# New order, engine, slot and filler tables for a fixed list of 2793 steps: attention followed by a two-layer MLP on one Trainium2 core

## Chip, cores and metric

One core of a Trainium2 chip runs the whole program. The metric is device microseconds of one execution, given as the median of the runs; one further execution was taken by the hardware profiler, and all rows below are from it.

## What is computed

The input has batch 4, 8 heads, 576 positions and head size 64. A small network of 32 hidden units makes a bias from the distance of two positions; the bias is the same for all batches. The result of the attention goes, token by token (2304 tokens of width 512), through a layer of width 2048 with a leaky step.

```python
scores = scale * np.matmul(q, k.transpose(0, 1, 3, 2))
...
x = (psi_rel / psi_i)[..., None]
h = np.maximum(x @ w1 + b1, 0.0)
bias = h @ w2
scores = scores + bias.transpose(2, 0, 1)[None, :, :, :]
...
attn = np.exp(scores)
attn = attn / (np.sum(attn, axis=-1, keepdims=True) + 1e-09)
attn_out = np.matmul(attn, v)
...
h = x @ w_in
g = np.maximum(h, 0.0) + alpha * np.minimum(h, 0.0)
return (g @ w_out).astype(np.float32)
```

## The kernel before

**The work and its tiles.** The program is written as 2793 steps; a step is one instruction or a short run of them on one engine (a matmul group, an elementwise operation, a DMA).

- 36 bias tiles (`bias_tile`, L472). Each takes four relu images ("H" steps, on ACT L485, DVE L482 or POOL L488), one PE group (L503) into a PSUM tile S or O, one eviction ("ev", ACT L513 or DVE L514) and one DMA to a scratch in HBM (`scr`).
- Weight preparation (`weights`, `halves_of`): for each of eight pairs of hidden blocks the weights are loaded, their bits are put together on DVE (L679, L682), the maximum is found, and a high and a low f16 half are written. The same splitting is done to q, k (`qk_turn`, L586 on PE, then L592 on ACT and L593 on DVE, or L597 on either for batch 0) and v (`v_rows`).
- 32 attention units (`unit`): for two heads and a range of rows, scores on PE (L611 in f32 for batch 0, L612 in f16 for batches 1 to 3) into S or O, a minimum on DVE (L823), the exponential on ACT (L826), the row scale (L829, L831), the division (L846, L847 for batch 0; L836, L837 and L839 for the others), a transposition (PE L855 with ACT L865 for batch 0, a transposing DMA L842 into the tile `at` for the others), the product with v on PE into A (L884 or L876), and an eviction of A in two parts by ACT (L902) and DVE (L904) into `x`.
- Nine chunks of 256 tokens (`chunk`, `layer_pair`), each with eight pairs of hidden blocks: a first-layer group of 24 matmuls into H (L954), two ACT (L961) and two DVE (L962) steps that read H, a high and a low half of the result (L965, and L966 on DVE or L967 on POOL), and a second-layer group of 12 matmuls into O (L973). O gathers all pairs of an output group. Chunks 0 and 1 are split into four output groups each, the seven others are one group each: 15 output groups. The second-layer group of the last pair is two steps of six matmuls, one for each half of O, and each half is then read by one ACT or DVE step (L935, L936; L939 where it is added to an earlier group).

**PSUM.** O is one tile of two halves of 512 f32, S are two tiles of 1024 f32 (O also serves as a third S slot), A is one tile of 512 f32 and H one tile of two halves of 256 f32.

**What sets the order.** Nothing is decided at run time but the waits. `Planner.plan` takes three tables written out in the file. `ISSUE` lists the numbers of the steps in the order in which they are issued, each engine taking its own steps from it in this order; a suffix .1 or .2 picks the second or third engine of those that the step may run on. `SLOT` gives each of 1115 buffers the slot that it lies in. `IDLE` lists steps of PE with a number of filler matmuls (L1025, 512 columns, into H's tile) that are issued just ahead of them.

```python
for b, n in zip(bufs, SLOT.split(), strict=True):
    b.slot = int(n)
...
for x in ISSUE.split():
    n, a = (x + ".0").split(".")[:2]
    o = self.ops[int(n)]
    o.eng, _, o.alt = o.alts[int(a)]
```

The two halves of the last second-layer group and their readers are declared as apart from each other: step `t` of PE writes `(ob, t)`, and reader `t` waits for `(ob, t)`.

```python
for t in range(2):
    PE(lambda t=t: m2([t]), 1320, ky + 0.0015, [gg, w_s[fp, 1]], [(ob, t)])
```

Of the kernel before, what the change touches and what calls it, by code (L numbers as in the profile page):

```python
# [34 lines left out]
0 2 1 3 4 5 6 9 10 11 13 12 193 7 8 441 442 16 14 15 17 19 443 194 205 195 23 71.1 70.2 444 206 69 105 445 72.1 107 446 18 24 25 26 27 28 29 207 114  # L35
73 113.2 112.2 30 31 197 32 153 20 154 111 208 198 155 49 156 447 157 160 115 104 106.2 199 161 21 50 211 108 22 48 162 56.1 74 51.2 163 200 76.2 77
448 109 52 662 78 35 57.2 79.2 36 80 164 196 53 39 58.2 212 40.1 213 661.2 214 158 116 55 175 159 81 176 165 215 663 59 91.2 660 93.2 166.1 219 60 209
110 664 90.2 41.1 92 94 177 178 179 180 98 181 54 665.1 189 97.1 100 220 190 216 182 82 201 99.2 217 218 183 184 42 101 167 919 920 168 221 62.1 222
102 656 169 654 653 223 921 33 227.1 655.2 95.1 202 203 170 922 171 34 172 657 43.1 44 65 45 64.2 923 658 103 37 204 210 83 63.1 224 38 84.1 75 251 66
173 46 86.2 926 225 927 187 928 924 625.2 226 627.1 85 626.2 228 87 117 61 614 229 929 119 188.1 628.2 930 612.2 925 47 88.1 629 230 67 252 253 120.1  # L40
121 630 231 255 118 659 232 185 233 234 646 235 122 931 239 254 244 237.1 186 631 932 246 933 191 259 613 611.2 615 96 240 934 647 620.2 256 192 269
68 238 649 935 616 245 648.2 123.1 247 650 619.1 633.1 666 260 621.2 634.1 936 632 651 89 617 618.2 622 635 937 257 636 241 128 127.1 126 258 652 125
124 637 606 270 271 605.1 604 248 129 607.1 608 667 272 236 261 668 242 623 669 938 263 262 130 670.2 609.1 480 140.2 671 264 939 249.1 265 267.1 481
672.1 139 147.2 142 149 273 141.2 266 484 143 148 940 943 134 277 274 144 610 146.1 639 275 150 485 135 281 638 642.1 640.2 276 133 482 641.1 944 643
697 132.2 342 136 624 688 282 151 690 278 131 673 689 283 279 145 137.1 691.2 152 343 284 483 486.1 698.1 692 280 285.1 268 487 696.1 286 138 695.2
491 644 677.1 699 693.1 676 346 488 675 287 700 354 288 489 289 674.2 344 290 291 726 490 725.2 347 292 345 723.1 678 348 250 683.1 355 645 494 941
293 350 492 681 682.1 684 679 349 304 493 685 358.1 724 356 711.2 686 495 942 712 727 498 351 511 499 710.2 709.2 305 352 496 728 497 357 719 713 353
512 359 733.1 717.1 694 360 309 500 701 716 306 501 687 310 515 714 680 311 505 718 506 729 361 513 720 362 313 507.1 703.1 363 243 731.1 502 503 704
516 514 705 702 314 721 302.1 364 315 504 321 517.1 730 525 365 307 312 303 366 706 316 518 707 368 295 542 526 174 370 519 732.1 529 715 530 527 722
508 522 528 543 531.1 708 317 738.1 740 369 734 297 509 371.1 322 375 298 532 533 546 547 536 735 544 520 523 510 737 556 739.1 736 323 545 521 372  # L50
318 324 296 573 537 319 373 741 320 308 548.1 524 742 379 387 534 535 374 549 553 376 325.1 557 550 560 326 327 538 561 554 558 559 562.1 328 377 329
330 380 331 555 299 332 333 743 551 381 563 574 552 300 378 567 335 587 577 539 578 575 576 382 568 744 336 337 540 564 388 579.1 565 383 758 772 773
301 569 745 566 338 391.1 541 389 580 339 746 340 584 570 748 384 412 341 747 390 585 581 385 582 749 586 750.1 759 367 787 571 408 572 386 583 751
762 392 760 755 774 393 413 761 588 763 775 414 756 589 764.1 765 394 757 752 766 415 416 395 420 396 788 590 591 753 397 776 398 409 399 777.1 791
401 778 801 754 769 592 767 410 789 792 402 417 418 411 779 780 781 768 815 421 770 449 771 790 424.1 422 802 419 816 817 593.1 423 425 594 595 426
793.1 805 803 830 427 794 450 334 596 294 403 428 818 429 430 804 431 432 598 597 806 819 404.1 461 405 599 844 400 600 807.1 808 820 406 455 433 782
436 798 456 809.1 434 799 795.1 451 457 810 812.1 452 453 796 783 785 407 800 813 814 821 784 786 858 601 797 454 467 917 945 946 947 948 437 949 950
473 822.1 602 474 823 462 435 811.1 475 468 476 477 831 603 834 463 859 464 824 832 951 833 438 835 836 837 458 825 845 478 860 846 2150 841 828 952
838 848 957.1 839 459 826 842 953 954 955 847 861 469 956.1 849 850.1 851 958 982 460 829 862 827 918 959 960 873 843.1 2153 852 983 855 984 985 840
2151 887 853 961 962 963 901 2152 854 863.1 470 2154 856 864 874 2167 465 857 865.1 2158 2161 875 2155.1 2156.1 479 877 964 866 876 965 888 966 967  # L60
878 968 969 867.1 970 889 891 879.1 971 880 2159 868 2160 2162 2163 902 2164.1 890 892 972 973 893.1 976 1022 894 974 975 986 471 988 989 979 869 977
980 978 2170 881 884 898 439 895.1 1036 871 440 981 899 2171 2173 896 900.1 2172 2174 872 885 897 886 903 2175.1 1023 904 916 1024 2176.1 2178 1025
1026 1027 1028.1 882 1029 1037 2179 883 990 991 992 1330 1331 1332 1030 1333 466 2207 993.1 2157 1040 1334 1038 1337 1338 905 906 1055 2166 1031 1069
1339 907 908 987 2181 1041 909 2180 1039 1340 2182 2165 2169 2190 870 1033.1 994.1 1034 1042 2183.1 1043 1044.1 1045 472 1341 910 2191 1032 1047.1
1056 1057 1035 2193 2192 2168 911 1046 1059 1048 1070 2194 1335 1336 2195.1 1088 1071 912 2198 913 2177 1073 1356 914 1342 1102 2184.1 995.1 1060 2227
1058 1061 1062 2196.1 2201 1072 1074 1343 1075 1063.1 1357 2185 2187 1066.1 915 1116 1358 1359 1344 2199 1345 1049 1064 1089 1067 2188 2202 2200 1076
2203.1 1065 1346 1090 2186 2204 2189 1080.1 1092 2210 1117 1347 1348 2213 1132 1103 1081 1077.1 1093 1106 1068 1082 1118 2211 1104 1078 1050 1107 2214
1349 1091 2212 1079 1146 1105 1051 1133 1136 1052 2215.1 1053 1019 1108.1 1137 2218 1054 1109 1094.1 1095 1160 2221 1119 1134 2219 996 1099 2197 1100
1113.1 1161 2205 1096.1 2206 997 1114 1097 1101 1120 1121.1 1122 2222 2208 998 2209 1123.1 1147 1350 999 1000 1001 2220 1115 1002 1162 1083 1124
2216.1 1003 1110.1 1135 1004 1148 1098 1138 1005 1139 1360 1149 1006 1086 2232 1111 2223.1 1126 2233 1007 2235 1163 1140 1150 1013 1351 1125 1112 1141  # L70
1008 2217 1142 1361.1 1362 1151 2234 1152 1009 1143 2236 2224 2237 1084 1010 1144 2226 2240 1011 1363 1087 1164 1153 2225 2229 1165.1 1364 1154 1176
2238.1 1014 1157.1 1012 1016 2241 2243 1368.1 1365 1190 1158 1155 1366 1367 1085 1015 1017 1145 1166 2244 1018 2228 1352 1156 2231 1127 1167 1353 1177
1128 1130 1209 2242 1178 2239 1129 1223 1354 1168 1131 1355 2251 1369.1 1370 2254 1170 1180 1169 2245 1191 1371 2246 1372 1194 1393 1179 1430 1181
2252 2248 1159 1373 1182 1394 1374 1375 1376 1195 2250 1377 1378 2247 1379 1395 1183 2253 1380 1187.1 1184.1 1192 1384 1385 2255 1396 1242 1381 1188
2259 2256 2249.1 1382 1387 2260 2262 1386 1193 1189 1397 1185 1383 2261 2263 1399 1196.1 1400 2257 1210 1211 1401 1020 1402 1388 1212 2270 1213 1197
2264 1198 1398.1 1389 1390 1391 1405.1 1256 1171 1172 1392 1214 1403 1186 1739 1740 2265.1 1741 1201 1199 1742 1202 1224 1227 1215.1 1404 2271 2258
1225 1203 1743 1216 1200 2272 2273 1406.1 2274 1228 2275.1 1243 1226 1173 1246 1229.1 1746 1174 1230 1175 2278 1270 1247 1744.1 1407 1021 1244 2276.1
1234.1 1257 1408 1409 1217 1218 1220 1260 1410 1271 1411 1412 1413 1261 1221 2279 2281 2266 1219 1747 1748 1204 1245 1414 1415 1416 1248 1417 1749
1222 1272 1286 2267 1273 1249 1231 1205 2280 1274 2282 1421 1422 1232 2289 2292 1258 1233 1235 1750 1236 1207 1300 1423 2268 1424 1259 1418 1262.1
2269 1206 2290 1314 2293 2277 1263 2283 1419 1420 1275 1250.1 1765 1751.1 1208 2291 1427 2284 1752 2297 1251 1428 1425 1253 1237 1238 1429 1276 2298  # L80
# [997 lines left out]
```

## Time and profile before

| what | value |
|---|---|
| runs | 707.54, 706.51, 704.47 us; median 706.51 |
| profiled execution | 706.55 us, of which the span from first to last instruction is 704.8 |
| mean granted TensorE clock | 0.994 |
| busy share of the span | PE 95%, DVE 70%, ACT 57%, POOL 25% |
| filler matmuls | 112, busy 35.0 us, the last at 145.5 us |

PE busy includes the fillers. A row of a wait names the engine that waited, the step that waited by its output tile and line, and what released it.

### The profile page before, as it was taken

How to read it: one execution, taken by the hardware profiler on the slowest of the kernel's cores; microseconds unless marked ns; L12 is line 12 of the kernel's file. 1: busy time of each engine (PE TensorE's matmuls, PEld its weight loads, DVE VectorE, ACT ScalarE, POOL GpSimd, SP SyncE). 2: the span in 40 equal slices, each digit the busy share in tenths (PEclk: the TensorE clock that was granted, in tenths of full speed). 3: DMA queues.
4: the chain of work that ended last, by engine and by line, in shares of the span. 5: the costliest groups of instructions: out<-in, count | busy, mean ns of one | idle time of the engine just before them, and what ended most of it. 6: DMA issues, size and time to landing. Idle time of an engine off the chain costs nothing.

```text
span 704.8 us, 15254 instructions
## 1 busy us (share of the span) xinstructions
PE 668.1 (95%) x5728; PEld 422.9 (60%) x5728; DVE 495.7 (70%) x1214; ACT 400.5 (57%) x824; POOL 174.2 (25%) x235
## 2 busy tenths in 40 slices
PE   7998889989999989999999999999999999999997
PEld 2454435556755656566666666666566566666664
DVE  3799999998767878798867786777668556123342
ACT  3897999886667656646565565474546352121211
POOL 1544434431320221222213212322122212111000
PEclk9999999999999999999999999999999999999999
DMA  8998998767479899999999969998998844200000
GB/s 201 273 300 303 298 314 292 253 179 206 103 167 212 176 224 200 176 222 218 210 195 190 191 180 216 203 193 190 188 200 175 178 86 82 59 30 1 31 1 31
DMA packets 234342, 125.89 MB, mean 179 GB/s; under 512 B 202636, under 2 KB 202652, under 8 KB 234268
## 3 DMA queue, kind: packets, MB, share of 16 engines
q1 hardware_dynamic: 234136, 124.91, 77.1%
q8 instruction: 45, 0.74, 0.4%
q14 instruction: 29, 0.24, 0.1%
q10 hardware_dynamic: 132, 0.00, 0.0%
HBM read 73.88 MB, written 15.61 MB: 127 GB/s over the span
## 4 chain that ended last, share of the span: by engine, by line
PE 73%; DVE 11%; ACT 6%; issue 4%; DMA 4%; POOL 1%; SPq 0%; DVEq 0%; ACTq 0%; POOLq 0%
PE H L954 24%; PE O L973 24%; PE A L876 6%; PE S L612 5%; DVE fg L823 3%; PE A L884 2%; PE S L503 2%; PE S L586 2%; DMA at<-a 2%; PE S L611 1%; ACT at L485 1%; PE S L855 1%; DVE five L682 1%; ACT fg L513 1%; PE H L1025 1%
## 5 line engine op out<-in xcount | busy, mean ns | idle before, releaser
L954 PE MATMUL H<-x,win 128*128 128x256 f16 x1728 | 200.8, 273 | 1.4 <-DVE mg L962 1.2
L973 PE MATMUL O<-wout,mg 128*128 128x512 f16 x864 | 197.9, 379 | 2.6 <-DVE mg L939 1.2
L954 PEld LDWEIGHTS <-win 128*128 128x128 f16 x1728 | 166.7, 98 | 35.9 <-issue 8.1
L961 ACT ACTIVATE mg<-H,sm 128x256 f32<-128x256 f32 x144 | 63.9, 469 | 153.2 <-PE H L954 138.7
L973 PEld LDWEIGHTS <-mg 128*128 128x128 f16 x864 | 82.1, 98 | 95.6 <-issue 7.6
L962 DVE SCALAR_TENSOR_TENSOR mg<-H,sm,mg 128x256 f32<-128x256 f32 x144 | 65.9, 478 | 96.1 <-ACT mg L961 96.1
L826 ACT ACTIVATE fg<-fg,st 128x576 f32<-128x576 f32 x144 | 110.5, 769 | 32.9 <-DVE st L823 23.9
L823 DVE CUSTOM_DVE_ANT_0 fg<-S,fg 128x576 f32<-128x576 f32 x125 | 92.4, 750 | 15.9 <-PE S L612 15.0
L967 POOL TENSOR_TENSOR mg<-mg 128x512 f16<-128x512 f32 x39 | 46.9, 1203 | 158.0 <-DVE mg L965 67.0
L839 DVE SCALAR_TENSOR_TENSOR a<-fg,st,a 128x576 f16<-128x576 f32 x74 | 63.8, 865 | 22.7 <-ACT a L837 11.3
L836 POOL TENSOR_SCALAR a<-fg,st 128x576 f16<-128x576 f32 x42 | 34.0, 810 | 116.7 <-DMA at<-a 51.1
L612 PE MATMUL S<-qk 64*128 64x288 f16 (+1 forms) x684 | 54.9, 284 | 3.1 <-ACT at L865 1.6
L876 PE MATMUL A<-at,five 128*64 128x256 f16 (+3 forms) x720 | 51.6, 288 | 1.3 <-DVE x L904 1.3
L612 PEld LDWEIGHTS <-qk 64*128 64x128 f16 (+1 forms) x720 | 33.5, 96 | 22.8 <-issue 16.9
L876 PEld LDWEIGHTS <-five 128*64 128x64 f16 (+1 forms) x720 | 36.4, 109 | 14.9 <-issue 11.7
L829 POOL TENSOR_SCALAR st<-st 128x2 f32<-128x2 f32 (+1 forms) x48 | 14.5, 303 | 115.3 <-ACT fg L826 95.8
L503 PE MATMUL S<-at,w2b 128*32 128x79 f32 (+39 forms) x492 | 36.6, 343 | 4.9 <-ACT at L485 2.3
L485 ACT ACTIVATE at<-cst 128x432 f32<-128x432 f32 (+17 forms) x53 | 33.0, 654 | 13.8 <-DVE cst L433 5.9
L1025 PE MATMUL H<-sm 128*128 128x512 f16 x112 | 35.0, 425 | 0.9 <-DVE sm L413 0.9
L846 POOL TENSOR_SCALAR fg<-fg,st 128x576 f32<-128x576 f32 x30 | 24.7, 834 | 35.8 <-PE S L611 13.6
L503 PEld LDWEIGHTS S<-at,w2b 128*32 128x32 f32 x492 | 19.0, 112 | 20.7 <-issue 6.4
L839 DVE SCALAR_TENSOR_TENSOR cst<-fg,st,cst 128x576 f16<-128x576 f32 x34 | 28.1, 826 | 4.3 <-ACT cst L837 4.0
(160 smaller groups left out, 908.6 us busy)
## 6 DMA issues: line engine op xcount, KB each, us to landing
fg<-scr SPq DMA_DIRECT2D x64, 576.0 KB, 4.7
scr<-fg SPq DMA_DIRECT2D x36, 295.5 KB, 5.7
x<-in_moe_w_in_dram SPq DMA_DIRECT2D x12, 512.0 KB, 5.5
x<-in_moe_w_out_dram SPq DMA_DIRECT2D x10, 512.0 KB, 5.3
fg<-scr SPq DMA_DIRECT2D x32, 144.0 KB, 4.3
out_dram<-mg SPq DMA_DIRECT2D x18, 256.0 KB, 2.5
five<-in_q_dram SPq DMA_DIRECT2D x32, 128.0 KB, 4.3
five<-in_k_dram SPq DMA_DIRECT2D x32, 128.0 KB, 3.5
```

The costliest lines, as they stand in the source:

```text
L503: nc.tensor.matmul(ps.t[32 * gl:32 * gl + 32, c:n], lhsT=w2b, rhs=x, start=True, stop=True)
L612: return [(lambda a, dst=dst, zq=zq, zk=zk, i=i: nc.tensor.matmul(dst(a), lhsT=tr16(qt)[at, 0, pr, zq, lo:lo + n], rhs=tr16(qt)[at, 1, pr, ...
L823: V(lambda x=x, sl=sl, st=st, ls=ls: nc.vector.tensor_tensor_reduce(out=in_halves(ls[x]()), in0=halves(sl[x].t), in1=in_halves(ls[x]()), s ...
L826: A(lambda x=x, st=st, ls=ls: nc.scalar.activation(ls[x](), ls[x](), AF.Exp, bias=st.t[:, x:x + 1], scale=-1.0, accum_out=st.t[:, 2 + x:3 ...
L839: V(lambda x=x, rec=rec, ls=ls, a16=a16: nc.vector.scalar_tensor_tensor(a16.t[:, 640:640 + S], ls[x](), rec(), a16.t[:, 0:S], op0=ALU.mult ...
L876: nc.tensor.matmul(ps.t[64 * hh:64 * hh + 64, 0:w], lhsT=v5[0:hi, zv, n, 2 * pr + hh, :], rhs=at16(at)[0:hi, 5 * za + n, 320 * hh:320 * hh ...
L954: nc.tensor.matmul(hb.t[:, f, :], lhsT=win[:, fp, zw, kb, P * f:P * f + P], rhs=x[:, zx, kb, :], start=(n == 0), stop=(n == 11))
L961: A(lambda f=f: nc.scalar.activation(gf(f), hb.t[:, f, :], AF.Copy, scale=cu[:, f:f + 1]), 470, ky, [hb, t_sig], [(g, f)])
L962: V(lambda f=f: nc.vector.scalar_tensor_tensor(gf(f), hb.t[:, f, :], cs[:, f:f + 1], gf(f), op0=ALU.mult, op1=ALU.max), 475, ky, [hb, t_si ...
L967: ("POOL", 1210, lambda: nc.gpsimd.tensor_tensor(gv(1), g.t, gv(0), op=ALU.subtract))], ky, [g, (gg, 0)], [(gg, 1)], tag="g1", cont=True)
L973: nc.tensor.matmul(ob.t[:, t, :], lhsT=gg.t[:, zg, f, P * t:P * t + P], rhs=wout[:, fp, zw, f, :], start=(first and f == 0 and (zg, zw) == ...
L1025: nc.tensor.matmul(idle, lhsT=zero.broadcast_to((P, P)), rhs=zero.broadcast_to((P, 512)), start=True, stop=True)
```

## The change

All three tables are replaced; no other line of the file is touched, and the 2793 steps and their dependences are the same. The title of the change says that the tables were searched with engines taking turns on each PSUM tile.

```diff
@@ -32,118 +32,118 @@
 ISSUE = """
-0 2 1 3 4 5 6 9 10 11 13 12 193 7 8 441 442 16 14 15 17 19 443 194 205 195 23 71.1 70.2 444 206 69 105 445 72.1 107 446 18 24 25 26 27 28 29 207 114
-73 113.2 112.2 30 31 197 32 153 20 154 111 208 198 155 49 156 447 157 160 115 104 106.2 199 161 21 50 211 108 22 48 162 56.1 74 51.2 163 200 76.2 77
...
+0 2 9 10 3 11 4 13 12 15 5 14 19 104 106 6 7 107.1 8 16 205 206 193 105.2 108 113 114.1 20 21 22 111.2 17 71.1 194 112 23 115 24 25 48 207 26 70.2 27
+28 55.2 208 72 197 29 69 73 30 441 31 109.1 32 116 195 74.1 153 154 198 155 35 37 156 76.1 51.1 79.2 50.1 49.1 36.1 219 39 52 77.2 442 196 58.2 38.1
...
 SLOT = """
-0 0 5 0 2 2 2 2 1 5 6 0 2 0 7 0 4 5 6 1 6 5 3 0 2 2 8 3 4 5 1 1 4 1 6 3 4 1 2 1 2 5 6 2 3 2 0 4 1 0 2 6 0 3 2 0 6 1 4 2 0 1 4 3 0 1 2 2 7 6 3 1 5 0 5
...
+0 0 6 0 0 0 1 2 0 6 4 5 1 1 2 3 4 2 6 1 8 5 4 2 6 2 5 1 2 0 3 2 6 1 6 0 4 1 6 1 2 4 0 2 2 6 4 0 5 1 9 0 5 3 2 0 3 2 3 0 1 0 4 0 2 6 4 2 9 2 4 1 5 0 7
...
 IDLE = """
-7:12 442:1 444:2 73:6 115:3 108:2 52:5 80:2 59:2 664:1 94:4 170:3 45:2 87:1 629:1 122:5 650:2 622:1 636:1 129:1 671:5 481:3 643:3 136:2 692:3 699:4
-678:2 685:6 727:2 713:2 506:3 706:2 526:5 741:3 557:2 327:1 395:1 780:1 802:5
+7:9 108:4 115:1 73:4 35:11 444:2 59:1 168:1 94:1 101:4 657:6 45:1 66:4 229:2 122:1 934:1 650:4 622:2 636:1 129:3 608:1 671:3 150:4 643:1 136:3 692:1
+699:5 678:1 287:2 685:2 495:5 713:2 720:6 543:3 537:6 557:3 329:1 568:2 774:2 802:4 426:1
 """
```

Counted over the whole tables, with each number looked up in the list of steps:

- The order of 411 steps of PE stays the same but for local swaps: 298 of them keep a common order. Of DVE's 1070 steps 358 do, of ACT's 655 it is 264, of SP's 426 DMA issues 244.
- Steps per engine go from 1070 to 1064 on DVE, 655 to 652 on ACT and 231 to 240 on POOL. Within that, relu images go from 72, 33, 39 (ACT, DVE, POOL) to 66, 38, 40, and bias evictions from 28 ACT and 8 DVE to 24 and 12.
- 707 of the 1115 slots differ.
- The fillers go from 112 to 121.
- At the start, the steps that scale the constant table (15 for L433, 14 for L432) are issued ahead of the copy of alpha (8, L426) and its followers, where they were behind them; the first bias group is 108 where it was 73.
- Of the 30 readers of O at the ends of the 15 output groups, 15 stood in the list right behind the group's last matmul step, with no step of PE in between; now 10 do. In the eight groups of chunks 0 and 1 it is 7 of 16 before and 2 of 16 now.
- For each of the 24 units whose tile `at` comes by transposing DMA, the matmul time that the list puts between the issue of the last transfer and the product with v (by the durations that the kernel's steps carry) goes from a median of 7.5 us to 6.1. Before, four units had under 4 us: 0.0, 0.8, 2.7, 3.5. Now it is seven: 0.0, 0.0, 0.8, 2.2, 3.4, 3.5, 3.9.
- Ahead of the first first-layer group (step 2150) DVE has 333 steps in place of 327: five more relu images, four more bias evictions, two more copies of q and k, one more maximum over q or k (L554), and a mixed remainder of six fewer, most of them one-column scale steps. ACT has 196 in place of 202, POOL 86 in place of 83, and PE the same 113.
- Of the 15 output groups, the number that have both an ACT and a DVE reader goes from 5 to 2.

## Rows read from the trace of the kernel before

**Rows 1.** Windows: busy us of each engine (x instructions), clock, DMA share, GB/s.

```profile
0.00:30.00 30.00, 25.04 (x229) 10.25 (x230) 15.05 (x39) 16.72 (x26) 10.37 (x19) 0.94 1.00 229
30.00:167.10 137.10, 122.90 (x1212) 67.99 (x1211) 130.45 (x319) 123.57 (x226) 53.93 (x71) 0.99 0.88 270
167.10:700.20 533.10, 520.13 (x4292) 344.68 (x4290) 349.51 (x858) 259.53 (x574) 109.94 (x147) 1.00 0.74 153
```

**Rows 2.** Windows of the filler matmuls (L1025) alone: PE, PEld, clock, DMA.

```profile
0.00:30.00 30.00, 13.82 (x39) 3.94 (x40) 0.94 1.00 229
30.00:167.10 137.10, 21.19 (x75) 6.08 (x73) 0.99 0.88 270
```

**Rows 3.** Timeline of PE at the first MLP matmul.

```profile
167.06 2.79 PE L954 MATMUL H<-x,win 128*128 128x256 f16 x24
```

**Rows 4.** Waits of PE from 167 us to the end: total, times, longest.

```profile
PE S L612 <- ACT at L865: 1.6, 1, 1.6
PE S L586 <- DVE qk L593: 1.6, 1, 1.6
...
PE A L876 <- DVE x L904: 1.3, 2, 0.9
PE O L973 <- DVE mg L939: 1.2, 1, 1.2
PE H L954 <- DVE mg L962: 1.2, 3, 0.5
PE O L973 <- ACT mg L935: 1.1, 1, 1.1
...
PE O L612 <- DVE mg L939: 0.3, 1, 0.3
```

**Rows 5.** Timeline of the last output group.

```profile
697.60 2.55 PE L973 MATMUL O<-wout,mg 128*128 128x512 f16 x11 [0.29 <-DVE mg L966]
700.18 0.75 DVE L936 TENSOR_SCALAR mg<-O,sm 128x512 f32<-128x512 f32 x1 [2.64 <-PE O L973]
...
700.97 0.69 ACT L935 ACTIVATE mg<-O,sm 128x512 f32<-128x512 f32 x1 [5.53 <-DVE mg L936]
```

**Rows 6.** Timeline of one first-layer result H, two of its readers.

```profile
642.95 0.48 DVE L962 SCALAR_TENSOR_TENSOR mg<-H,sm,mg 128x256 f32<-128x256 f32 x1 [3.46 <-ACT mg L961]
643.47 0.47 ACT L961 ACTIVATE mg<-H,sm 128x256 f32<-128x256 f32 x1 [0.55 <-DVE mg L962]
```

**Rows 7.** Timeline of ACT behind an output reader.

```profile
201.60 0.69 ACT L935 ACTIVATE mg<-O,sm 128x512 f32<-128x512 f32 x1 [3.35 <-PE O L973]
...
205.29 0.68 ACT L865 ACTIVATE at<-S 128x640 f32<-128x640 f32 x1
```

**Rows 8.** Timeline of DVE behind an output reader.

```profile
254.17 0.75 DVE L939 SCALAR_TENSOR_TENSOR mg<-O,sm,mg 128x512 f32<-128x512 f32 x1 [4.67 <-PE O L973]
254.84 0.81 DVE L593 SCALAR_TENSOR_TENSOR qk<-S,sm,qk 128x576 f16<-128x576 f32 x1
```

**Rows 9.** Timeline of the start: const table lands, its scaling, first bias step.

```profile
7.83 0.13 PEld L425 LDWEIGHTS A<-cst,alr 16*128 16x128 f32 x1 [2.52 <-DMA cst<-in_const_dram]
...
8.57 0.51 DVE L432 TENSOR_SCALAR cst<-cst,sm 128x576 f32<-128x576 f32 x1
...
9.32 1.81 ACT L485 ACTIVATE at<-cst 128x512 f32<-128x512 f32 x3 [5.92 <-DVE cst L433]
```

**Rows 10.** Groups of DVE up to 167.1 us: busy us, mean ns, idle before.

```profile
L482 DVE TENSOR_SCALAR at<-cst 128x448 f32<-128x448 f32 (+11 forms) x26 | 13.4, 525 | 0.2
...
L514 DVE TENSOR_SCALAR fg<-S,cst 128x591 f32<-128x591 f32 x6 | 5.3, 880 | 0.0
```

**Rows 11.** Groups of DVE over the whole span.

```profile
L593 DVE SCALAR_TENSOR_TENSOR qk<-S,sm,qk 128x576 f16<-128x576 f32 x22 | 17.8, 812 | 3.1 <-ACT qk L592 3.1
...
L554 DVE TENSOR_REDUCE sm<-five 128x1 f32<-128x1280 f32 x3 | 4.4, 1480 | 0.1
```

**Rows 12.** Tile at, 240 to 600 us: transposing transfers, issue to landing.

```profile
DMA to landing us min/median/max: 3.0/3.6/6.6
```

206 rows, old and new, of tables (ISSUE, SLOT) are left out of this document.

## The prediction

> **What bounds the kernel now.** I read the busy time by stage first, then the waits of PE in the late stage, then the timelines around the longest of them. The stages are cut at 167.06 us, where the first MLP matmul runs [rows 3]. Ahead of it no matmul of the MLP can fill PE, and DVE and ACT set the pace: from 30 to 167.1 us DVE is busy 130.45 of 137.10 us and ACT 123.57 [rows 1]. PE's share there is padded: the fillers take 13.82 us before 30 us and 21.19 after it, and none runs after 167.1 [rows 2]. From 167.1 to 700.2 us PE is busy 520.13 of 533.10 us with no filler, at a granted clock of 1.00, so 2.4 GHz, while DVE has 183 us to spare [rows 1]. So the late stage can lose at most the 13.0 us in which PE waits. The rest is matmul work that the change leaves as it is, and a tail of 4.6 us behind the last matmul (704.8 less 700.2).
>
> **Who makes PE wait.** Seven kinds of wait carry 8.3 of these us [rows 4]. Three end directly on a step that reads an output group: 1.2 and 0.3 us on L939, 1.1 on L935. Two end on a step that stood behind such a reader in its engine's queue. ACT's L935 had waited 3.35 us for the second layer, and L865, which frees the S tile, came only at 205.29, three and a half us later [rows 7]; PE waited 1.6 us for it. DVE's L939 had waited 4.67 us, and L593, which frees the next S tile, stood right behind it [rows 8]; PE waited 1.6 us again. That makes 5.8 us around O. The other two, 1.3 and 1.2 us, end on the last readers of A and H, L904 and L962.
>
> The reason shows in two places. The last output group is two halves; the code lets the reader of half 0 go when the first six matmuls are done. Five of the eleven matmuls that begin at 697.60 belong to half 0, so it is complete at about 697.60 + 5/11 x 2.55 = 698.8. Its reader starts at 700.18, with DVE idle, when PE is through with half 1 too, and ACT's reader of half 1 starts at 700.97, 0.04 us after DVE's ended at 700.93 [rows 5]. H shows the same between ACT and DVE: 642.95, then 643.47, the second ACT step waiting for a DVE step that reads the other half [rows 6]. So engines do take turns on a whole PSUM tile, and an order that counts on reading half 0 early puts its reader too far forward in an in-order queue, with other work stuck behind it.
>
> **The change part by part.**
>
> *Output readers.* The new list has 2 readers of O in chunks 0 and 1 right behind the last matmul, where there were 7 of 16. That is where the waits around O lie. I let the same share of the waits by turns go: 5/7 of 8.3 us is 5.9 us. Bounds: 0, if other steps merely take these places, and 13.0, if PE never waits again. The value lies nearer the middle because readers were moved, not removed; those that stay keep their waits.
>
> *Start.* The constant table lands at 7.83, and its scaling starts at 8.57 behind the copy of alpha; ACT's first relu follows at 9.32 [rows 9]. Issued first, scaling can start 0.74 us earlier, and so can everything that DVE and ACT do. I take 0.7 us; bounds 0 (weights still land when they did) and 0.74.
>
> *Load ahead of the MLP.* DVE gets five relu images at 0.525 us and four evictions at 0.880 [rows 10], two copies (not among DVE's rows shown; nearest, the 0.812 us of L593, which reads the same tile) and one maximum of 1.480 [rows 11]: 2.6 + 3.5 + 1.6 + 1.5 = 9.2 us. The mixed remainder of six fewer steps I leave out. ACT and POOL change by less, in opposite senses. I charge nothing for it, because DVE's idle time ahead of 167.1 us is 14.95 + 6.65 = 21.6 us [rows 1], of which at least 21.6 - 8.6 = 13.0 lies behind the scaled table; the new list starts DVE on relu images and evictions in just that time. If this cover is not there, it costs up to 9.2 us; if it is filled and the idle time falls further, the first MLP matmul could come up to 13.0 - 9.2 = 3.8 us sooner.
>
> *Fillers.* Nine more. They stand ahead of steps that wait on DVE or ACT in the early stage, so they cost nothing; without that cover it is 9 x 13.82/39 = 3.2 us at most [rows 2], well inside the case above.
>
> *Slots and alternatives.* A slot has no duration; it only says who waits for whom. More H results are read ACT, DVE, ACT, DVE in the new list (29 of 72, against 19), each step 0.52 us after the one before [rows 6]. This is hidden by the second-layer group of 12 matmuls that PE has in the meantime. I take 0.
>
> *Transfers.* The transposing transfers land 3.0 to 6.6 us after issue, 3.6 in the median [rows 12]. With 3.6, the four close units of before would fall short by 0.1 + 0.9 + 2.8 + 3.6 = 7.4 us, and yet no wait of PE for such a transfer is among the waits of the late stage; the list's distance is evidently not all the time that there is. The seven of now would fall short by 0.2 + 3.6 + 2.8 + 3.6 + 0.1 + 1.4 = 11.7 us. I charge nothing, as before, and keep the other end: with the longest landing of 6.6 us it is 32.4 us against 19.4, so 13.0 more.
>
> Sum, on the profiled execution's own time: 706.55 - 5.9 - 0.7 = 699.95, so 700.0 us (a span of 698.2). The median of the runs, 706.51, is the same within 0.1 us, so no correction is needed.
>
> **A rule weighed against the row.** The late reader at 700.18 is the row on which the term of 5.9 us rests [rows 5]. The Trainium skill, in "PSUM — Partial Sum Buffer", section "PSUM bank collisions raise a hardware error", wants engines kept apart by bank and by group of 32 partitions, and lets them work on different banks at once. A half of O fills one bank there, so by this rule a reader of half 0 need not wait for the matmuls of half 1; the readers were then rightly placed, the term would be 0 and the sum 705.8 us. For H, whose halves share a bank, the rule and the row [rows 6] agree. On O the trace differs, and I go by the trace.
>
> **The rivals.**
>
> *DVE becomes the bound ahead of the MLP.* The 9.2 us fall where DVE is already full, everything behind moves, and 700.0 becomes 709.2, or 706 with a third of it covered by idle time. For it: 95% busy from 30 to 167.1 us [rows 1]. Against it: DVE's 15 us of idle time before 30 us. This counts as no clear change.
>
> *The waits only move.* The new order removes none of PE's waits by turns, because a reader of half 0 was not held up by them, or because something else is now stuck behind the readers: 706.55 - 0.7 = 705.85. For it: 10 of 30 readers still stand right behind the last matmul. Against it: the 1.4 us between 698.8 and 700.18 [rows 5]. The rule of the Trainium skill in "PSUM — Partial Sum Buffer" named above would end at this time too.
>
> *Both stages tighten.* PE's waits go almost wholly and the first MLP matmul comes sooner: from 700.0 down to 706.55 - 13.0 - 0.7 = 692.9, of which I take 695.
>
> *The other side: transposed tiles land late.* The products with v wait on `at` in the seven close units. At its price of 13.0 us the time is 713.0. It decides against the forecast once the seven lose 10 us together, 1.4 us each; then the sum passes 710. For it: the median distance falls by 1.4 us and three units now have under 1 us. Against it: four close units cost nothing so far.
>
> **How the numbers follow.** Chances: forecast 0.52 (own range 696.5 to 703), both stages tighten 0.12, DVE bound 0.16, waits only move 0.08, transfers late 0.12. A measurement of this kernel can tell about 0.5% from no change, so the marks are 703.0 and 710.0. Below 703.0 are the forecast and the tightening: 0.64. Between lie the DVE case and the moved waits: 0.24. Above: 0.12. The range of 694 to 709 leaves out the late transfers, the upper edge of the DVE case and a little at the low end, together 2 in 10.
>
> **What would show it.** Right: the waits that end on L935, L939, and on L865 and L593 behind them, fall from 5.8 us to under 2; PE's idle time from the first MLP matmul to the last falls from 13.0 to about 7; the first MLP matmul still runs at 166 to 167 us; the table is scaled at about 7.9 us. Wrong: a first MLP matmul past 170 with DVE full before it; waits of L876 for transfers; or the same waits by turns at other lines. The weakest step is the charge of nothing for DVE's 9.2 us: the stage ahead of the MLP is the one that the rows say least about.

## The result and the profile after

The changed kernel takes 698.48 us (median of 13 runs, 696.34 to 703.98), the kernel before in the same session 706.53 (13 runs, 704.07 to 710.8). The ratio is 0.9885, with a 95% interval of 0.9861 to 0.9908: 8.1 us less, where 6.5 were forecast. The two profiled executions, 706.55 and 696.34 us, lie 10.2 us apart; the second is the lowest of its 13 runs.

The windows of the changed kernel, cut at its first MLP matmul (165.56 us) and at the end of its last (689.95), answer to [rows 1]; columns as there.

```profile
0.00:30.00 30.00, 24.12 (x215) 11.46 (x215) 19.55 (x47) 12.32 (x19) 8.06 (x15) 1.00 0.93 215
30.00:165.56 135.56, 121.87 (x1237) 66.69 (x1237) 130.26 (x311) 119.60 (x218) 56.83 (x74) 1.00 0.88 282
165.56:689.95 524.39, 519.55 (x4292) 343.59 (x4290) 346.59 (x852) 265.90 (x582) 115.78 (x155) 1.00 0.75 154
```

The third line is the one to read. The late stage has the same 4292 matmuls, busy for 519.55 us against 520.13, but it is 524.39 us long and not 533.1. So PE's idle time there fell from 13.0 to 4.8 us. The 10.2 us between the two executions are 8.7 us of late stage, 1.5 us by which the first MLP matmul came sooner, and nothing at the tail (4.55 us against 4.6).

The waits of PE from 165.5 us on are all that is left of [rows 4].

```profile
PE S L612 <- DVE qk L593: 2.2, 3, 1.2
PE A L876 <- DMA at<-cst: 0.6, 1, 0.6
PE A L464 <- DVE x L904: 0.5, 1, 0.5
PE H L954 <- DVE mg L962: 0.5, 1, 0.5
PE S L586 <- DVE st L823: 0.4, 1, 0.4
PE O L973 <- DVE mg L966: 0.3, 1, 0.3
```

No wait ends on a reader of the output tile O any more (L935, L936, L939), nor on L865. L593 is still there, but not behind such a reader: at the longest of its waits (253.24 us) DVE ran L593 first and L939 after it, the other way round than in [rows 8]. From the timeline of DVE there:

```profile
252.38 0.81 DVE L593 SCALAR_TENSOR_TENSOR qk<-S,sm,qk 128x576 f16<-128x576 f32 x1
...
253.50 0.74 DVE L939 SCALAR_TENSOR_TENSOR mg<-O,sm,mg 128x512 f32<-128x512 f32 x1
```

The start answers to [rows 9]. The timelines of ACT, DVE and PE:

```profile
7.92 1.28 ACT L485 ACT_TABLE_LOAD   x1 [7.92 <-DMA cst<-in_const_dram]
9.22 0.66 ACT L485 ACTIVATE at<-cst 128x432 f32<-128x432 f32 x1
...
7.95 0.30 DVE L433 TENSOR_SCALAR cst<-cst,sm 128x144 f32<-128x144 f32 x1 [1.10 <-DMA cst<-in_const_dram]
8.16 0.52 DVE L432 TENSOR_SCALAR cst<-cst,sm 128x576 f32<-128x576 f32 x1
...
10.38 0.48 PE L503 MATMUL O<-at,w2b 128*32 128x159 f32 x2
```

The kernel before, beside [rows 9]:

```profile
9.00 0.29 DVE L433 TENSOR_SCALAR cst<-cst,sm 128x144 f32<-128x144 f32 x1
...
12.80 0.34 PE L503 MATMUL S<-at,w2b 128*32 128x79 f32 x1
```

The table is scaled by two steps, which have changed places. They run from 7.95 to 8.68 us, and ran from 8.57 to 9.29: 0.6 us sooner. The first bias group on PE (L503) comes 2.4 us sooner, at 10.38 against 12.80. ACT gains only 0.10 (9.22 against 9.32), because the small exponential that had fetched its function table at 1.90 us now stands late in the order: the table load of 1.28 us has moved to 7.92, behind the transfer of the constants. The Trainium skill, "ScalarE: Activation LUTs", section "What ACT_TABLE_LOAD costs", gives about 1283 ns for the load; the row agrees.

The fillers (L1025) of the two windows ahead of the MLP, 11.87 and 24.45 us, answer to [rows 2]:

```profile
0.00:30.00 30.00, 11.87 (x34) 3.46 (x34) 1.00 0.93 215
30.00:165.56 135.56, 24.45 (x88) 7.17 (x87) 1.00 0.88 282
```

### The profile page after: what moved, and what is told of

Read it like the earlier page. It is cut to its first block, busy times and chain, and to the rows that moved or that the text cites. A ratio compares the mean times of both kernels' runs of the same rounds, so it can differ in the third digit from the quotient of the medians.

```text
span 694.5 us, 15288 instructions
## 1 busy us (share of the span) xinstructions
PE 665.5 (96%) x5737; PEld 421.7 (61%) x5737; DVE 496.4 (71%) x1208; ACT 399.1 (57%) x820; POOL 180.7 (26%) x244
## 4 chain that ended last, share of the span: by engine, by line
PE 72%; DVE 12%; DMA 6%; issue 4%; ACT 3%; POOL 2%; SPq 0%; ACTq 0%; DVEq 0%; POOLq 0%
PE H L954 25%; PE O L973 24%; PE S L612 7%; PE A L876 6%; DMA at<-a 2%; PE A L884 2%; PE S L586 2%; PE S L503 1%; DVE fg L823 1%; DVE five L682 1%; DVE wout L682 1%; DVE qk L593 1%; DVE at L482 1%; PE S L855 1%; DMA five<-in_k_dram 1%
## 5 line engine op out<-in xcount | busy, mean ns | idle before, releaser
L954 PE MATMUL H<-x,win 128*128 128x256 f16 x1728 | 200.7, 273 | 0.7 <-DVE mg L962 0.5
L973 PE MATMUL O<-wout,mg 128*128 128x512 f16 x864 | 197.7, 379 | 0.3 <-DVE mg L966 0.3
L954 PEld LDWEIGHTS <-win 128*128 128x128 f16 x1728 | 166.5, 98 | 33.9 <-issue 6.8
L962 DVE SCALAR_TENSOR_TENSOR mg<-H,sm,mg 128x256 f32<-128x256 f32 x144 | 66.8, 479 | 105.7 <-ACT mg L961 105.5
L961 ACT ACTIVATE mg<-H,sm 128x256 f32<-128x256 f32 x144 | 64.8, 470 | 134.1 <-PE H L954 115.2
L973 PEld LDWEIGHTS <-mg 128*128 128x128 f16 x864 | 82.6, 98 | 92.5 <-issue 3.8
L826 ACT ACTIVATE fg<-fg,st 128x576 f32<-128x576 f32 x144 | 110.6, 769 | 29.0 <-DVE st L823 23.8
L823 DVE CUSTOM_DVE_ANT_0 fg<-S,fg 128x576 f32<-128x576 f32 x127 | 93.6, 751 | 15.7 <-PE S L612 14.6
L967 POOL TENSOR_TENSOR mg<-mg 128x512 f16<-128x512 f32 x41 | 50.1, 1222 | 114.1 <-ACT mg L965 45.2
L839 DVE SCALAR_TENSOR_TENSOR a<-fg,st,a 128x576 f16<-128x576 f32 x71 | 59.5, 840 | 19.8 <-POOL a L836 9.9
L612 PE MATMUL S<-qk 64*128 64x288 f16 (+1 forms) x696 | 56.6, 285 | 2.2 <-DVE qk L593 2.2
L829 POOL TENSOR_SCALAR st<-st 128x2 f32<-128x2 f32 (+1 forms) x54 | 17.3, 320 | 123.1 <-ACT fg L826 118.9
L485 ACT ACTIVATE at<-cst 128x528 f32<-128x528 f32 (+17 forms) x54 | 33.8, 659 | 10.2 <-PE S L503 7.4
L503 PE MATMUL S<-at,w2b 128*32 128x79 f32 (+37 forms) x462 | 32.9, 334 | 5.5 <-ACT at L485 1.9
L1025 PE MATMUL H<-sm 128*128 128x512 f16 x121 | 36.3, 412 | 0.9 <-DVE sm L413 0.9
L965 ACT ACTIVATE mg<-mg 128x512 f16<-128x512 f32 x40 | 24.9, 624 | 17.9 <-DVE mg L962 6.6
L839 DVE SCALAR_TENSOR_TENSOR cst<-fg,st,cst 128x576 f16<-128x576 f32 x37 | 32.0, 864 | 3.0 <-ACT cst L837 3.0
L488 POOL TENSOR_SCALAR at<-cst,npsi 128x416 f32<-128x416 f32 (+15 forms) x28 | 23.1, 827 | 41.6 <-PE S L503 24.0
```

What stands on the lines that cost most here:

```text
L503: nc.tensor.matmul(ps.t[32 * gl:32 * gl + 32, c:n], lhsT=w2b, rhs=x, start=True, stop=True)
L612: return [(lambda a, dst=dst, zq=zq, zk=zk, i=i: nc.tensor.matmul(dst(a), lhsT=tr16(qt)[at, 0, pr, zq, lo:lo + n], rhs=tr16(qt)[at, 1, pr, ...
L823: V(lambda x=x, sl=sl, st=st, ls=ls: nc.vector.tensor_tensor_reduce(out=in_halves(ls[x]()), in0=halves(sl[x].t), in1=in_halves(ls[x]()), s ...
L826: A(lambda x=x, st=st, ls=ls: nc.scalar.activation(ls[x](), ls[x](), AF.Exp, bias=st.t[:, x:x + 1], scale=-1.0, accum_out=st.t[:, 2 + x:3 ...
L839: V(lambda x=x, rec=rec, ls=ls, a16=a16: nc.vector.scalar_tensor_tensor(a16.t[:, 640:640 + S], ls[x](), rec(), a16.t[:, 0:S], op0=ALU.mult ...
L954: nc.tensor.matmul(hb.t[:, f, :], lhsT=win[:, fp, zw, kb, P * f:P * f + P], rhs=x[:, zx, kb, :], start=(n == 0), stop=(n == 11))
```

## The experiments

Twelve kernels, each timed against the kernel before on the same chip. The tables `ISSUE` and `IDLE` name a step by its number; a diff below shows moved steps one to a line, with what is left out marked by `...`. Some texts say up projection for the first-layer group (L954) and down projection for the second-layer group (L973). A scale chain is the short run of steps from L464 to L466 by which a maximum over all partitions is found. For each run this table gives the median, the ratio with its interval, and from its profile the first MLP matmul, PE's busy time in the late stage (first to last MLP matmul) and its idle time there, which is the stage's length less the busy time.

| kernel | median us | ratio | first MLP | PE busy | PE idle |
|---|---|---|---|---|---|
| before | 706.5 | 1 | 167.1 | 520.2 | 13.0 |
| changed | 698.5 | 0.9885 [0.9861, 0.9908] | 165.6 | 519.6 | 4.8 |
| 1 before, readers later | 700.2 | 0.9908 [0.9878, 0.9938] | 166.8 | 520.1 | 8.5 |
| 2 changed, readers early | 710.6 | 1.0052 [1.0025, 1.0079] | 167.1 | 525.0 | 14.8 |
| 3 changed start, old late stage | 710.8 | 1.0064 [1.0038, 1.0091] | 166.4 | 523.3 | 16.4 |
| 4 old start, changed late stage | 701.9 | 0.9935 [0.9913, 0.9958] | 166.1 | 522.5 | 8.2 |
| 5 changed, more fillers | 695.8 | 0.9847 [0.9819, 0.9875] | 166.4 | 519.7 | 5.5 |
| 6 changed, early table load | 697.6 | 0.9862 [0.9836, 0.9888] | 166.5 | 519.7 | 5.0 |
| 7 changed, ACT's readers early | 702.5 | 0.9930 [0.9905, 0.9955] | 165.7 | 520.5 | 10.4 |
| 8 changed, old fillers | 702.5 | 0.9933 [0.9907, 0.9958] | 168.4 | 520.1 | 6.6 |
| 9 as 1, three PE steps swapped | 701.0 | 0.9916 [0.9889, 0.9944] | 165.7 | 521.3 | 8.4 |
| 10 as 5 and 6, four PE steps swapped | 702.2 | 0.9928 [0.9906, 0.9950] | 165.3 | 519.3 | 9.7 |
| 11 changed, H read in pairs | 698.4 | 0.9884 [0.9856, 0.9913] | 166.1 | 521.2 | 5.5 |
| 12 changed again | 698.2 | 0.9883 [0.9854, 0.9913] | 165.8 | 519.4 | 4.4 |

**1. Before, with 16 readers later.** Each now stands one or two PE steps behind the last matmul step of its group; one of them (2169), and that last step (2165):

```diff
 2165
-2169
 2190
 ...
 1056
+2169
```

> The kernel before, with 16 of the 30 readers of the output tile (lines 935, 936, 939) moved later in the order, each behind one or two more PE steps after the last down projection of its group; engines, slots, fillers and everything else as before. Theory 1 (a reader that is queued too soon stands at the head of ACT or DVE until the whole tile is done, and holds up what PE wants next): PE's idle time between the first and the last MLP matmul falls from 13.0 to 7 to 9 us, the waits behind lines 865, 593, 935 and 939 go, ratio 0.9915 to 0.9945; the first MLP matmul stays at 167. Rival 2 (the waits only move to other steps): idle 12 to 13 us, ratio 0.998 to 1.002. Rival 3 (the gain of the change came from the stage ahead of the MLP, or from the order of the late stage as a whole): ratio 0.998 to 1.002 as well, with the readers' own waits gone.

The idle time fell to 8.5 us and the time by 0.92%. At the place of [rows 7] and of [rows 8] the timelines of ACT and DVE now read:

```profile
201.58 0.68 ACT L865 ACTIVATE at<-S 128x640 f32<-128x640 f32 x1
205.03 0.68 ACT L935 ACTIVATE mg<-O,sm 128x512 f32<-128x512 f32 x1
...
253.04 0.82 DVE L593 SCALAR_TENSOR_TENSOR qk<-S,sm,qk 128x576 f16<-128x576 f32 x1 [0.19 <-ACT qk L592]
253.78 1.40 DVE L939 SCALAR_TENSOR_TENSOR mg<-O,sm,mg 128x512 f32<-128x512 f32 x2
```

L865 runs at 201.58 and not at 205.29, and neither reader has waited for PE. Of the five kinds of wait that made up the 5.8 us around O only the 0.3 us on L939 is left. That is 5.5 us less, and the idle time fell by 4.5, so some of it came back elsewhere. From the waits of PE:

```profile
PE S L612 <- DVE st L823: 2.1, 4, 0.8
PE A L464 <- DVE sm L633: 1.2, 1, 1.2
PE A L466 <- DVE sm L465: 1.2, 1, 1.2
...
PE A L464 <- ACT mg L961: 0.7, 1, 0.7
...
PE O L612 <- DVE mg L939: 0.3, 1, 0.3
```

Sixteen moves among 2793 steps, with slots, engines and fillers as before, give most of the gain. Rival 2 falls, and so does rival 3 as far as these 6.6 us go; the step from 0.9908 to the changed kernel's 0.9885 lies within both intervals.

**2. Changed, with 13 readers back.** One of them:

```diff
 2186
 ...
+2188
 1075
 ...
 1065
-2188
```

> The changed kernel, with 13 readers of the output tile moved back to where the table of before has them: right behind the last down projection of their group, or one PE step behind it; everything else as changed. Theory 1: about 5 us of the gain is lost, PE's idle time in the late stage rises from 4.9 to 9 to 11 us, ratio to the kernel before 0.994 to 0.998. Rivals 2 and 3 (the readers' places are not what pays): idle stays at 5 to 6 us and the ratio at 0.987 to 0.990.

All of the gain is lost, and more: by the medians 12 us above the changed kernel. Theory 1 has the direction and less than half of the size. The waits of DVE from 166 us on show the hold itself:

```profile
DVE mg L939 <- PE O L973: 5.9, 3, 2.5
...
DVE mg L936 <- PE O L973: 4.9, 3, 2.5
```

They were 0.8 and 0.6 us in the changed kernel. What comes of one of them, from the timelines of PE and DVE:

```profile
215.75 2.32 PE L973 MATMUL O<-wout,mg 128*128 128x512 f16 x10
...
218.11 1.41 DVE L939 SCALAR_TENSOR_TENSOR mg<-O,sm,mg 128x512 f32<-128x512 f32 x2 [2.48 <-PE O L973]
...
219.71 0.27 DVE L904 SCALAR_TENSOR_TENSOR x<-A,sm,x 128x64 f16<-128x64 f32 x1
...
220.03 0.27 PE L464 MATMUL A<-cst,sm 128*1 128x128 f32 x1 [1.96 <-DVE x L904]
...
222.28 0.58 PE L466 MATMUL A<-cst,sm 1*128 1x1 f32 x2 [0.56 <-DVE sm L465]
222.79 4.95 PE L954 MATMUL H<-x,win 128*128 128x256 f16 x24
```

DVE stands idle for 2.48 us at the reader until PE is through with the tile, L904 behind it is late, and PE waits for L904. Then comes a second cost. The 24 matmuls of the up projection (L954) take 4.95 us at 222.79; the same group takes 2.78 elsewhere in this trace. The granted clock of that window is in the last column but two:

```profile
220.00:225.00 5.00, 4.41 (x26) 2.83 (x27) 4.93 (x15) 2.92 (x6) 0.69 (x1) 0.54 0.54 88
225.00:230.00 5.00, 5.00 (x56) 3.83 (x55) 1.95 (x6) 2.61 (x8) 2.05 (x4) 0.78 1.02 181
```

0.54 means that most of it ran at 1.2 GHz. It happened again at 260 to 265 us (0.66). So between the two profiled executions 9.9 us of the loss are idle time and 5.4 are the same matmuls run slower; with 1.5 us ahead of the MLP they make 16.8, more than the 12 of the medians, because the one profiled here (713.13 us) is among the slower of its 12 runs.

**3 and 4. The two stages apart.** The tables are joined at the first MLP matmul, 3 and its reverse 4:

```diff
-steps ahead of 2150 in the order of before (863), their slots and fillers
+steps ahead of 2150 in the changed order (873), their slots and fillers
 2150 and all steps left, in the order of before
```

> The changed kernel's table up to the first MLP matmul (873 of its steps, with its slots and its fillers), then every step that is left in the order of before. Four slots of fg and some names of slots had to differ. Theory 1: the first MLP matmul at 165.6 and the late stage with 12 to 14 us of idle PE, as before: 1 to 2 us sooner, ratio 0.997 to 0.999. Rival 3 (what is done ahead of the MLP pays off later too, since more of the attention work is behind it): idle of the late stage falls to 8 or less, ratio 0.991 to 0.994.

> The reverse: the table of before up to the first MLP matmul (863 steps, with its slots and fillers), then what is left in the changed order. Theory 1: first MLP matmul at 167, idle PE in the late stage 5 to 7 us, 6 to 8 us sooner in all, ratio 0.989 to 0.992. Rival 3: the late stage needs the new start, idle 9 us or more, ratio 0.995 to 1.000.

Both expectations are off, and 3 is slower than the kernel before where it was to be faster. The reason is the same: the seam costs. Steps that the one order has ahead of 2150 and the other behind it stand together there, 14 in 3 and 24 in 4. Behind it PE's first scale chain waits for L904, which on DVE stands behind other steps and their waits (timelines of PE in 3, then in 4):

```profile
174.16 0.27 PE L464 MATMUL A<-cst,sm 128*2 128x128 f32 x1 [3.76 <-DVE x L904]
```

```profile
172.47 0.37 PE L464 MATMUL A<-cst,sm 128*2 128x128 f32 x1 [2.61 <-DVE x L904]
```

Each is followed by a stretch at a lower clock (0.66 at 175 to 180 in 3, at 170 to 180 in 4). Without the 2.61 us, kernel 4 would have 5.6 us of idle time in its late stage; the changed kernel has 4.8. So, by this subtraction, the changed late stage carries its gain with the old start, and the changed start brings the old late stage nothing: the late stage of 3 has the waits of [rows 4] on L865, L593, L935 and L939 unaltered (1.6, 1.6, 1.1, 1.2 us).

**5. Changed, with more fillers.**

```diff
 IDLE
-7:9
+7:16 360:5
```

> The changed kernel with 12 more filler matmuls where PE stood idle ahead of the MLP: 16 rather than 9 ahead of the transpose of alpha (line 425, 3.4 us of waiting for its transfer) and 5 ahead of the scale of the sixth weight pair (line 464, 1.22 us of waiting for line 689). Two of three profiled executions with this order ahead of the MLP showed the granted clock down at 5 to 15 and at 120 to 125 us. Theory (the clock that falls behind these waits is lost time): no slice of the first 160 us under 0.98, the first MLP matmul at 165.0 to 165.8, the median 0.5 to 2 us under the changed kernel's 698.48, ratio 0.9858 to 0.9880. Rival (what falls ahead of the MLP is caught up by the slack there): ratio 0.9875 to 0.9895.

The lowest median of all, 695.8 us. Its profile shows no slice of the first 160 us under full clock, as expected, but the first MLP matmul is at 166.4, not sooner. That execution (697.91) is one of its slower ones, so where the 2.7 us under the changed kernel's median would come from is not seen. Its interval overlaps that of the changed kernel: probably faster, not shown.

**6. Changed, with the early table load.** The steps at the head:

```diff
 2
+1
 9
 ...
 18
-1
 80
```

> The changed kernel with the one-element exponential of the start (line 416) ahead of ACT's first relu again, as in the kernel before, so that ACT's table is loaded at 1.9 us and not at 7.92 behind the transfer of cst. Theory: ACT's first relu starts at 8.6 to 8.7 and not at 9.22, the first bias group on PE 0.3 to 0.6 us sooner, of which nothing or up to 0.6 us reaches the end: ratio 0.987 to 0.989. Rival (the start decides the end one to one): ratio 0.9875 and first MLP matmul 0.6 sooner. Neither can be told from no change by the time alone; the profile's start and first MLP matmul tell.

From the timelines of ACT and PE:

```profile
1.90 1.28 ACT L414 ACT_TABLE_LOAD   x1 [1.90 <-issue]
...
8.75 0.66 ACT L485 ACTIVATE at<-cst 128x432 f32<-128x432 f32 x1 [5.35 <-DVE cst L432]
...
8.60 1.89 PE L1025 MATMUL H<-sm 128*128 128x512 f16 x4
10.42 0.48 PE L503 MATMUL O<-at,w2b 128*32 128x159 f32 x2
```

ACT is 0.47 us sooner and the first bias group, against the expectation, is not (10.42 against 10.38): four fillers stand in front of it. The first MLP matmul, 166.5, gains nothing. The theory's end without gain holds, and the ratio of 0.9862 is not clear of the changed kernel's.

**7. Changed, with nine of ACT's readers early.** One of them:

```diff
 2247
 ...
+2249
 1376
 ...
 1193
-2249
 2253
```

> The changed kernel with nine readers of the output tile that run on ACT moved back right behind the last down projection of their group, six of them past one to three PE steps and past 1 to 6 ACT steps each; the readers on DVE stay where the change has them. Theory 1 as it was forecast (a reader queued too soon is a hold on whichever engine it stands): PE's idle time in the late stage rises from 4.8 to 7 to 9 us, ratio 0.992 to 0.995. Rival (only DVE, which is busy for 66% of the late stage, can't make up for being held, ACT at 51% can): idle 4.5 to 6, ratio 0.987 to 0.9905.

Seven of the nine change their place; two stood there already. The idle time rises to 10.4 us, the time by 4 us, so the rival falls: a hold on ACT costs as well. The longest new wait ends a chain that runs over ACT, DVE and PE (timelines of the three):

```profile
265.01 1.26 ACT L935 ACTIVATE mg<-O,sm 128x512 f32<-128x512 f32 x2 [3.17 <-PE O L973]
266.17 0.77 ACT L826 ACTIVATE fg<-fg,st 128x576 f32<-128x576 f32 x1
...
267.81 0.17 DVE L829 TENSOR_SCALAR st<-st 128x2 f32<-128x2 f32 x1 [3.19 <-ACT fg L826]
267.89 0.48 DVE L962 SCALAR_TENSOR_TENSOR mg<-H,sm,mg 128x256 f32<-128x256 f32 x1
...
268.42 2.78 PE L954 MATMUL H<-x,win 128*128 128x256 f16 x24 [2.02 <-DVE mg L962]
```

ACT waits 3.17 us at the reader, the softmax step L826 behind it is late, DVE stands 3.19 us at L829 for that, L962 behind L829 is late, and PE waits 2.02 us for the tile that L962 reads. In the changed kernel the three L826 steps start at 261.38 to 262.91, ahead of the reader at 263.67. The Trainium skill, "PSUM — Partial Sum Buffer", section "Engine vs sequencer instructions", says that the queues of ScalarE, VectorE and GpSimd are strictly first in, first out; the rows agree, twice in one chain. That ACT waits in total for its readers longer in the changed kernel than before (16.8 against 11.6 us) fits this: the length of a hold says little, and what stands behind it decides.

**8. Changed, with the fillers of before.** The changed order with the IDLE table of before.

> The changed kernel with the filler table of before (112 fillers ahead of the same steps as there, where these now stand). Theory (fillers cost and bring next to nothing): ratio 0.987 to 0.991, first MLP matmul within 1 us of 166. Rival (with the fillers in the wrong gaps the granted clock falls more often ahead of the MLP): first MLP matmul at 168 or later, ratio 0.992 to 0.997.

The rival holds in time, 4 us, but not by its cause. The first MLP matmul comes at 168.4, later than in any of the eleven profiles of both orders with their own fillers (165.6 to 167.1), while the granted clock ahead of the MLP is down only at the start (0.92 and 0.74 between 5 and 15 us), no more than in others. By the table, 2.2 of the 4 us lie ahead of the MLP (168.4 against a mean of 166.2 for this order), and 1.8 are idle time behind it. That fillers in the wrong gaps stand in the way of work is likely and not shown; through which step was not traced.

**9. As 1, with three PE steps swapped.**

```diff
+1089
 1345
...
+2266
 1257
...
+1991
 2063
```

> The kernel before with the 16 readers moved later (the experiment above) and three PE steps put ahead of a step at which PE still waited there: a score step ahead of the maximum of v (216.47, 1.23 us for line 633), the first output matmuls of a pair ahead of a score step (285.66, 0.83 us), an attention product ahead of a score step (525.54 and 526.22, 0.78 us). Nothing else is changed. Theory (the waits that the 16 readers left over are as easily covered by other ready work): PE's idle time in the late stage 8.5 to 5.5 to 7 us, time 1.5 to 2.8 us under the 16 readers alone, ratio 0.985 to 0.989, which is the changed kernel's own gain out of 19 moves. Rival (they only move): idle 8 to 9, ratio 0.989 to 0.993.

**10. As 5 and 6, with four PE steps swapped.** Put ahead of the steps that wait: 839 ahead of 959, 2251 ahead of 1177, 1237 ahead of 1287, 2289 ahead of 1421.

> The changed kernel with the 12 more fillers, the early table load, and four PE steps put ahead of a step at which PE waited in its late stage (0.53 us at 169.43, 1.23 at 253.24, 0.36 at 289.73, 0.98 at 301.62 and 302.34). Theory: of those 3.1 us half go, idle 4.8 to 3 to 4 us; with the fillers 2 to 4 us under the changed kernel, ratio to before 0.982 to 0.986. Rival (projections put forward hold the attention work up): idle 5 or more, ratio 0.985 to 0.990.

In 9 the rival holds: the idle time stays (8.4 against 8.5 us). In 10 it is the rival's way, and further than it went (0.9928 where it had at most 0.990). The idle time is nearly double that of 5 and 6: the up projection that was put ahead waits for its own tile, and the next down projection for a reader of the output tile (timeline of PE):

```profile
252.59 2.78 PE L954 MATMUL H<-x,win 128*128 128x256 f16 x24 [1.17 <-DVE mg L962]
...
258.73 1.46 PE L973 MATMUL O<-wout,mg 128*128 128x512 f16 x6 [2.52 <-DVE mg L939]
```

The 1.23 us at 253.24 became 1.17 and 2.52.

**11. Changed, with H read in pairs.** In 15 of 72 layer pairs:

```diff
+ACT L961, second half
 DVE L962, first half
-ACT L961, second half
```

> The changed kernel with the steps that read the up projection's tile (lines 961 on ACT, 962 on DVE) in the order ACT, ACT, DVE, DVE wherever the change lists them in turn (15 of 72 layer pairs). Theory: the order inside H is worth nothing, since PE waits for H for 0.5 us in all: ratio within 0.002 of the changed kernel, idle 4.5 to 5.5. Rival (the turns are worth something): idle 6 to 8, ratio 0.990 to 0.993.

No difference, as the theory has it. The test is half of what it was meant to be: the changed list has 29 layer pairs in turn, and 14 of them still are in this kernel.

**12. The changed kernel again.**

> The changed kernel once more, unaltered, beside the three above on one chip. Expected: median 696.5 to 699, first MLP matmul between 165.5 and 167.1 as in the six profiles with its first 873 steps, and the granted clock down for some 4 us between 5 and 15 us, as in four of them. If that fall is there, the first profile of it, without one, was a lucky execution; if not, the spread has another cause.

The median is the same; the clock's fall at the start is absent, against the expectation, so by its own words the spread has another cause; which one stays open. Of the seven profiles with this order and these fillers ahead of the MLP (changed, 2, 3, 6 but for one step, 7, 11, 12), five show the granted clock down between 5 and 15 us and two do not, and those two have the shortest spans (694.5 and 694.1). That is a hint only: 2, 3 and 7 are longer for other reasons, so it rests on 6 and 11 (695.9 and 697.4). One window of the changed kernel, and the same of kernel 6:

```profile
10.00:15.00 5.00, 4.84 (x61) 2.62 (x60) 2.52 (x8) 2.46 (x5) 1.40 (x3) 1.00 1.06 232
```

```profile
10.00:15.00 5.00, 4.76 (x59) 2.20 (x57) 2.55 (x8) 1.77 (x3) 1.28 (x2) 0.56 1.02 233
```

## Why the prediction was right, point by point

**Output readers, 5.9 us.** The mechanism was right and is shown from both sides: readers later in the old order take 4.5 us of idle time away, readers earlier in the changed order bring 9.9 back, and ACT's alone 5.6. The term was too small: the late stage lost 8.1 us of idle time and 0.6 of busy time. The seven kinds of wait of 8.3 us that it was worked out from did about as it said: 2.7 us are left (0.5 on L962, and 2.2 on L593 at other steps), so 5.6 went. That this lies so near 5.9 is partly luck, since 5/7 is a share of readers, and the waits around O went wholly. What it left out are PE's other waits in that stretch, 4.4 us, of which 1.8 are left. The larger ones, which [rows 4] does not show, in the kernel before:

```profile
PE S L612 <- DVE st L823: 1.4, 3, 0.8
...
PE A L466 <- DVE sm L465: 1.1, 1, 1.1
```

With L464 the scale chains made 2.5 us. In kernel 1 those are still there, and longer (L464 and L466: 3.3 us in all, L823: 2.1); in the changed kernel the chains wait 0.5 us and L823 0.4. How the search covered them was not taken apart: swapping single PE steps by hand (9, 10) did not do it.

**Start, 0.7 us.** The sooner start came (0.6 us for the scaled table, 2.4 for the first bias group, though only 0.10 for ACT, because of the table load), but not its worth. The first MLP matmul ran between 165.6 and 167.1 in seven profiles of the changed order ahead of the MLP (mean 166.2) and between 165.7 and 167.1 in four of the old one (mean 166.4). The 1.5 us between the first two profiles are spread between executions. So the sum of 700.0 came near 698.5 in part by luck: it took 0.7 us too much here, and 2.8 too little in the late stage (5.9 against 8.7 between the two profiles).

**DVE's load ahead of the MLP, nothing.** The weakest step by its own account, and right, and for its reason. DVE is busy for 149.81 us ahead of the MLP against 145.46, and all of these 4.4 us more lie in the first 30 us (19.55 against 15.05), in the idle time that was to cover them. The price of 9.2 us was too high as a whole because the mixed remainder, left out as small steps, gave back about half; the largest single piece is a weight maximum of 1.2 us (L686) that is now on ACT.

**Fillers, nothing.** Right for their number: with twelve more (5) nothing was lost. Wrong for their places, which were not priced: with the old table the changed order loses 4 us (8).

**H, slots, transfers, nothing.** H's order is worth nothing in the 15 pairs tried (11). Transfers cost 0.6 us of PE's wait, of a bound of 13.0. Slots were not tried alone.

**The rule on PSUM.** In the last group of the changed kernel the reader again starts only when PE is through with both halves, at 689.99 us against 689.95 (timelines of PE and ACT, for [rows 5]):

```profile
687.40 2.55 PE L973 MATMUL O<-wout,mg 128*128 128x512 f16 x11 [0.34 <-DVE mg L966]
...
689.99 1.26 ACT L935 ACTIVATE mg<-O,sm 128x512 f32<-128x512 f32 x2 [4.88 <-PE O L973]
```

Here the trace can tell more than the two start times. Engines let each other go by semaphores, counters that one raises and another waits for, and the trace records them. Of the twelve matmuls of this last group only the last raises PE's semaphore (it ends at 689.95; before, at 700.14). Before, L936 waits for that one, and L935 for the one that L936 raises. In [rows 6] the second L961 waits in the same way for the one that the first L962 raises. So nothing tells a reader that its half is complete: in these places the turns are in the program's own guards, which go by the whole tile. The row at 700.18, on which the term rests, is therefore no evidence on what the chip would allow, for or against the rule on banks that the prediction set against it; a program with a guard for each half was not run.

**The rivals.** That DVE becomes the bound and that transposed tiles are late did not come. That both stages tighten came in part: the late stage lost 8.1 of its 13.0 us, the stage ahead of it nothing clear of the spread. That waits only move is what PE steps swapped by hand did, not what the change did.

## What to carry to other kernels

A reader that is queued before its whole tile is done does not merely wait: it holds every step behind it on an in-order engine, and the cost is read from those steps, not from the reader's own wait; moving it later is cheap and can be done one reader at a time. A tuned order is a whole: a foreign start (kernel 4 beside the changed one, kernel 3 beside the one before), foreign fillers (8 beside the changed kernel) or four steps swapped by hand (10 beside 5 and 6) cost 3 to 6 us here. Before reading a microsecond out of one pair of profiles, look how far two executions of the same kernel lie apart.

## What the runs showed of the hardware

The granted clock can turn a short wait of PE into a longer loss. In the late stage it fell at waits of 1.96 and 2.19 us (2), of 3.76 and 1.57 us (3), of 2.61 us (4), of 1.59 us (9) and of 1.41 us (11). It did not fall at waits of 2.52 us (10), 2.02 us (7) and 1.62 us (before), so the length of one wait does not tell. In the five profiles with such a fall (2, 3, 4, 9, 11) the stage's matmuls took 521.2 to 525.0 us in all, against 519.3 to 520.5 in the others. Ahead of the MLP PE waits for alpha's transfer. In the seven profiles named under 12 the fall followed in the five with waits of 3.59 to 3.77 us and not in the two with 3.43 and 3.46; in the old order it came with 2.82 to 3.08 us (1, 4, 9). With seven more fillers ahead of that wait (5, 10) it was absent in both. The forecast had no term for this; in the late stage of the changed kernel's own two profiles it did not occur.
